# Weight loads of the opening that wait for an earlier landing

## The chip, the cores and the metric

The kernel runs on one core of one Trainium2 chip. The time is device microseconds (us) of one execution. A difference is measured as the median of several runs of each kernel. Beside the times there is a profile of one execution, which records every engine's instructions and every DMA packet.

## The reference

A gated linear recurrence over 768 steps for 4 batches and 8 heads of 48, followed by a feed-forward layer with weights of 384 x 2048 and 2048 x 384. Inputs and weights are drawn in double precision for the weights and in float32 for the rest.

```python
def _attn_ref(q, k, v, alpha):
    B, H, S, D = q.shape                      # 4, 8, 768, 48
    state = np.zeros((B, H, D, D), dtype=np.float32)
    y = np.zeros_like(q)
    for t in range(S):
        state = alpha[:, :, t, :, None] * state + np.einsum('bhd,bhe->bhde', k[:, :, t], v[:, :, t])
        y[:, :, t] = np.einsum('bhd,bhde->bhe', q[:, :, t], state)
    return y

def _moe_ref(x, w_in, w_out):                 # x (3072, 384)
    h = x @ w_in
    g = np.where(h >= 1, h, np.where(h <= -1, 0.0, (h + 1) ** 2 / 4.0))
    return (g @ w_out).astype(np.float32)
```

## The kernel before

The 3072 tokens are cut into 24 chunks of 128 steps, and the chunks into 8 groups of three. For each chunk DVE scans the gates (L478, L485), multiplies keys and queries by the products (L493, L510), TensorE (PE) turns the keys (L574), makes the scores (L589), the state's update (L602) and the outputs (L769). For each group follows one pass of the feed-forward layer: for each of 16 tiles of 128 hidden columns a product with w_in (L878 for group 0, L887 for the others), the activation on ACT and DVE (L918, L928), and a product with w_out (L960 for group 0, L969 for the others). Group 0 multiplies whole float32 numbers; the others use weights split into two parts.

The weights come as 64-bit words and are decoded on the chip. They are loaded in 16 pieces of 768 KB, eight of w_in and eight of w_out, each with two of the 16 tiles, by the function `weights` (the issue is L427). Decoding one piece takes two passes of ACT (L349, L357) and three of DVE (L365, L376, L388), in the piece's own buffer, `wt`. Each piece has a buffer of its own, so a weight load waits for no reader. A chunk needs three loads: the gates `raw_a` (L455, 258.5 KB, two buffers), keys and queries `raw_kq` (L458, 512 KB, two buffers) and values `both` (L465, 512 KB, three buffers); such a load waits until the chunk before it in its buffer has been used. From L402 on the splitting of some weights uses a DMA that adds, issued by POOL.

All loads are issued by SP, in one row, one after the other. An instruction of SP that waits holds up all that stand behind it. The order of all engines is worked out ahead by a planner (`Plan.order`): it gives each operation an engine, a start and an end from costs, and lets a load start only when the transfers before it have at most `DEPTH` = 3 us left to move (with `RATE` = 395 KB per us, about 1.2 MB). The instructions are then emitted in that order at L1043 and L1044, and each engine carries out its own in that order, whenever what it waits for is there. The planned starts themselves do not go into the program.

A load tells of its landing through one of eight semaphores, DMAHW0 to DMAHW7, which the loads take in turn. A load that takes a semaphore whose last user has not been waited for by anyone waits for that user first. So at most eight loads of SP are under way.

The loads of SP are counted here from 1, in SP's order. Load 1 is the first `raw_a`; loads 10, 12, 15, 17, 19, 21, 24, 25, 26, 28, 29, 30, 32, 33, 35 and 36 are the 16 weight loads. Load 22 is a `raw_kq`, loads 23, 27 and 31 are `both`. PE carries out products of zeros (L1020) in the opening, put there by the planner.

Of the kernel before, what the change touches and what calls it, by code (L numbers as in the profile page):

```python
# [29 lines left out]
MORE = 2  # L30
NV = 3
WARM = 10
LAG = 4.0
FETCH = 9
LOAD = 12.0
# [206 lines left out]
def gated_attention_ffn(ctx: ExitStack, tc: tile.TileContext, q, k, v, alpha, w_in, w_out, by, out):  # L242
# [3 lines left out]
    P = 128  # L246
# [57 lines left out]
    with ExitStack() as main:  # L304
# [31 lines left out]
        n_w = NW * DM  # L336
        whole_w = lambda t: t.rearrange("p a m -> p (a m)").bitcast(F32)[:, 0:n_w]

        def decode(u, which, raw, key):

            w = buf("stage", "w", [P, n_w], 2)
            bits = lambda: w().bitcast(I32)


            plan.op(
                "ACT",
                0.92,
                key,
                lambda: nc.scalar.activation(out=w(), in_=word(raw(), F32, 1), func=AF.Copy, scale=2.0**-112),  # L349
                [raw],  # L350
                [w],
            )
            plan.op(
                "ACT",
                0.92,
                key,
                lambda: nc.scalar.activation(out=word(raw(), I32, 0), in_=word(raw(), U32, 0), func=AF.Copy, scale=2.0**-29),  # L357
                [raw],
                [(u, which)],
            )  # L360
            plan.op(
                "DVE",
                0.56,
                key,
                lambda: nc.vector.tensor_scalar(  # L365
                    out=bits(), in0=bits(), scalar1=3, scalar2=None, op0=ALU.logical_shift_left
                ),
                [w],
                [w],
                port=True,  # L370
            )
            plan.op(
                "DVE",
                0.96,
                key,
                lambda: nc.vector.scalar_tensor_tensor(  # L376
                    out=bits(),
                    in0=word(raw(), I32, 1),
                    scalar=-0x80000000,
                    in1=bits(),  # L380
                    op0=ALU.bitwise_and,
                    op1=ALU.bitwise_or,
                ),
                [w, raw],
                [w],
                port=True,
            )
            add = lambda e: e.tensor_tensor(out=whole_w(raw()).bitcast(I32), in0=bits(), in1=word(raw(), I32, 0), op=ALU.add)  # L388
            plan.op("DVE", 0.98, key, lambda: add(nc.vector), [w, raw, (u, which)], [raw], port=True)

        def part_w(u, which, raw, parts, key):
            part = lambda a: parts().rearrange(PARTS[which])[:, a * n_w : (a + 1) * n_w]
            data = lambda: whole_w(raw())
            plan.op("ACT", 0.83, key, lambda: nc.scalar.copy(out=part(0), in_=data()), [raw], [parts])
            sub = lambda e: e.tensor_tensor(out=part(1), in0=data(), in1=part(0).bitcast(F32), op=ALU.subtract)
            if u < BYSUM:
                plan.op("ACT", 0.86, key, lambda: nc.scalar.mul(out=part(1), in_=part(0).bitcast(F32), mul=-1.0), [parts], [parts])
                plan.op(
                    "POOL",
                    1.0,  # L400
                    key,
                    lambda: nc.gpsimd.dma_start(out=part(1), in_=data(), accum_op=ALU.add),  # L402
                    [raw, parts],
                    [parts],
                    moved=P * n_w * 4,
                    land=0.8,
                    rate=Plan.SUM,
                )
                return
            plan.op("DVE", 0.95, key, lambda: sub(nc.vector), [raw, parts], [parts], port=True)  # L410
# [3 lines left out]
        def weights(u):  # L414
# [7 lines left out]
            for k, (t, src) in enumerate(((ti, w_in), (to, w_out))):  # L422
                plan.op(
                    "SP",
                    Plan.ISSUE,
                    fetch[k] + k * LAG,
                    lambda t=t, src=src: nc.sync.dma_start(out=t(), in_=src[u]),  # L427
# [4 lines left out]
            decode(u, "i", ti, ready + off("di", u))  # L432
            decode(u, "o", to, ready + LAG + off("do", u))

        def parts_of(u):
# [4 lines left out]
            part_w(u, "i", raws_w[u][0], wi[u], key + off("wi", u))  # L440
            part_w(u, "o", raws_w[u][1], wo[u], key + LAG + off("wo", u))

# [573 lines left out]
        def fill(n):  # L1016

            idle = pools["ps"].tile([P, 512], F32, name="ps", bufs=8)
            for _ in range(n):
                nc.tensor.matmul(out=idle, lhsT=zeros, rhs=nothing, start=True, stop=True)  # L1020

        plan.op("PE", 0.44 * WARM, -99, lambda: fill(WARM), mode="full")
        for u in range(NU):
# [3 lines left out]
        for j in range(NCH):  # L1027
# [6 lines left out]
            while at < len(segs) and first[at] + groups[at] - 1 <= done:  # L1034
# [3 lines left out]
                for f in range(NF):  # L1038
                    key = begin[at] + f * step[at]
                    second(segs[at], f, hidden(at, f, key), key + LAG)  # L1040
                at += 1
        with tc.manual_schedule():
            for o in plan.order():  # L1043
                o.emit()  # L1044


        near = pools["att"].tile([P, G, P], F32, name="ks", bufs=1)[:, 0, 0 : NCH * G]
# [197 lines left out]
```

## Time and profile before

| | us |
|---|---|
| median of three runs | 501.81 (501.47 to 501.83) |
| the profiled execution | 501.42 |
| its span, first to last instruction | 499.7 |
| PE busy over the span | 491.5 (98%) |
| DVE busy | 347.3 (69%) |
| ACT busy | 317.9 (64%) |

The profiled execution's time is its span and 1.7 us around it; it lies 0.39 us below the median. A share of busy time is a mean over stages. In the opening DVE and the DMA engines are busy nearly all the time, later PE alone is, so a change to the opening has to be read from the opening's own rows.

### The profile page before, as it was taken

What the parts mean: (1) busy time and instruction counts of PE and PEld (TensorE: products, weight loads), DVE (VectorE), ACT (ScalarE), POOL (GpSimd) and SP (SyncE); (2) the same over time, 40 slices, a digit from 0 to 9 for tenths busy, and PEclk for the clock granted to TensorE, in tenths of its full rate; (3) what the DMA queues carried; (4) which work ended last, traced back from release to release, by engine and by line L of the source; (5) the groups of instructions that cost most, each with busy time, mean ns of one, the idle gap of its engine ahead of it and who ended that gap; (6) DMA issues with size and microseconds to landing.
All of it is one profiled execution on the core that took longest, in us unless ns stands there. A gap on an engine that the chain in (4) does not pass through costs nothing.

```text
span 499.7 us, 11372 instructions
## 1 busy us (share of the span) xinstructions
PE 491.5 (98%) x4586; PEld 446.5 (89%) x4586; DVE 347.3 (69%) x609; ACT 317.9 (64%) x603; POOL 30.5 (6%) x70
## 2 busy tenths in 40 slices
PE   8899999999999999999999999999999999999996
PEld 3665656699999999999999999999999999999995
DVE  6998999998997866865866857767755635343332
ACT  3799998998765565565665655665565655555551
POOL 4211102211000000000000000000000000000000
PEclk9999999999999999999999999999999999999999
DMA  8999916878552531542434513434313201001001
GB/s 315 394 387 387 330 23 142 208 201 181 181 159 65 187 102 49 150 137 82 110 95 118 174 47 124 130 100 139 115 35 89 70 1 25 1 7 42 0 1 51
DMA packets 43336, 64.42 MB, mean 129 GB/s; under 512 B 21392, under 2 KB 30736, under 8 KB 43280
## 3 DMA queue, kind: packets, MB, share of 16 engines
q1 hardware_dynamic: 41840, 59.71, 37.4%
q0 software_dynamic: 1440, 3.93, 4.2%
q8 instruction: 38, 0.62, 0.5%
q14 instruction: 18, 0.15, 0.1%
HBM read 48.56 MB, written 9.18 MB: 116 GB/s over the span
## 4 chain that ended last, share of the span: by engine, by line
PE 94%; DVE 3%; issue 1%; DMA 1%; POOL 0%; ACT 0%; DVEq 0%
PE ps L969 36%; PE ps L887 35%; PE ps L878 6%; PE ps L960 6%; PE ps L769 5%; PE ps L602 3%; PE ps L589 2%; DVE inv L485 1%; DVE pre L478 1%; DMA raw_a<-in_al 1%; PE ps L574 1%; DVE inv L493 0%; DVE Q L709 0%; DVE Q L510 0%; DVE state L653 0%
## 5 line engine op out<-in xcount | busy, mean ns | idle before, releaser
L969 PE MATMUL ps<-gh,wt 128*128 128x384 f32 x1008 | 197.1, 340 | 0.0
L887 PE MATMUL ps<-xs,wt 128*128 128x384 f32 x1008 | 193.6, 335 | 0.0
L969 PEld LDWEIGHTS ps<-gh,wt 128*128 128x128 f32 x1008 | 177.7, 188 | 1.3 <-issue 0.2
L887 PEld LDWEIGHTS ps<-xs,wt 128*128 128x128 f32 x1008 | 176.7, 188 | 0.7
L928 DVE SCALAR_TENSOR_TENSOR gf<-gf,ps 128x384 f32<-128x384 f32 x128 | 70.6, 552 | 94.0 <-ACT gf L918 92.5
L918 ACT ACTIVATE gf<-ps,half_b 128x384 f32<-128x384 f32 x128 | 74.4, 582 | 83.4 <-PE ps L887 80.5
L937 ACT CAST gh<-gf 128x384 fp32r<-128x384 f32 x112 | 57.4, 513 | 59.0 <-DVE gf L928 49.7
L938 DVE TENSOR_TENSOR gh<-gf,gh 128x384 fp32r<-128x384 f32 x112 | 62.0, 555 | 33.3 <-ACT gh L937 32.6
L918 ACT ACTIVATE gf<-gf 128x384 f32<-128x384 f32 x128 | 67.2, 525 | 4.0
L635 ACT COPY both<-state 48x192 f32<-48x192 f32 x88 | 30.8, 350 | 10.5 <-PE ps L602 9.1
L960 PE MATMUL ps<-gf,wt 128*128 128x384 f32 x96 | 33.0, 488 | 0.4 <-PE ps L878 0.4
L878 PE MATMUL ps<-xs,wt 128*128 128x384 f32 x96 | 32.7, 489 | 0.1
L478 DVE TENSOR_TENSOR_SCAN pre<-raw_a,fwd 128x516 f32<-128x516 f32 x24 | 29.5, 1228 | 3.0 <-DMA raw_a<-in_al 2.7
L485 DVE TENSOR_TENSOR_SCAN inv<-raw_a,bwd 128x516 f32<-128x516 f32 x24 | 30.1, 1254 | 2.1
L769 PEld LDWEIGHTS ps<-Q,both 128*64 128x64 f32 x368 | 23.2, 138 | 7.2 <-issue 5.6
L960 PEld LDWEIGHTS ps<-gf,wt 128*128 128x128 f32 x96 | 18.0, 190 | 12.4 <-PE ps L878 0.8
L878 PEld LDWEIGHTS ps<-xs,wt 128*128 128x128 f32 x96 | 17.8, 190 | 11.9 <-ACT wt L357 0.4
L769 PE MATMUL ps<-Q,both 128*64 128x64 f32 x368 | 26.6, 225 | 0.0
L769 PE MATMUL ps<-other,both 128*64 128x64 f32 x368 | 26.6, 225 | 0.0
L501 POOL COPY meet<-inv 128x4 f32<-128x4 f32 x24 | 9.8, 408 | 258.3 <-DVE inv L485 258.3
L769 PEld LDWEIGHTS ps<-other,both 128*64 128x64 f32 x368 | 23.2, 138 | 0.0
L709 DVE TENSOR_TENSOR Q<-ps,mask 64x256 f32<-64x256 f32 x48 | 20.3, 423 | 3.6 <-ACT other L672 1.8
(62 smaller groups left out, 370.1 us busy)
## 6 DMA issues: line engine op xcount, KB each, us to landing
raw_kq<-in_kq SPq DMA_DIRECT2D x24, 512.0 KB, 5.2
both<-in_vl SPq DMA_DIRECT2D x24, 512.0 KB, 4.6
raw_a<-in_al SPq DMA_DIRECT2D x24, 258.5 KB, 3.3
wt<-in_w_out SPq DMA_DIRECT2D x8, 768.0 KB, 9.4
wt<-in_w_in SPq DMA_DIRECT2D x8, 768.0 KB, 8.4
out<-ot SPq DMA_DIRECT2D x24, 192.0 KB, 3.1
turned<-w SPq DMA_DIRECT2D x17, 256.0 KB, 2.2
ks<-turned SPq DMA_DIRECT2D x68, 64.0 KB, 2.6
```

The lines of the kernel that those rows point to most:

```text
L478: lambda: nc.vector.tensor_tensor_scan(flat(pre()), a[:, 0:n], flat(fwd), 0.0, ALU.mult, ALU.max),
L485: lambda: nc.vector.tensor_tensor_scan(flat(inv())[:, ::-1], a[:, 1 : n + 1][:, ::-1], flat(bwd)[:, ::-1], 0.0, ALU.mult, ALU.max),
L635: lambda r=r, to=to: nc.scalar.copy(out=to, in_=state[low[r], b]),
L769: nc.tensor.matmul(out=ps()[halves[r], to, halves[u]], lhsT=lhsT[:, u, r], rhs=x()[:, g, halves[u]], start=m + u == 0, stop=True, skip_gro ...
L878: nc.tensor.matmul(out=h(), lhsT=raw_in(f)[:, kt], rhs=whole_x(n)[:, kt].rearrange("p j t -> p (j t)"), start=kt == 0, stop=kt == KT - 1,)
L887: nc.tensor.matmul(out=h(), lhsT=win(f, w)[:, kt], rhs=xs[n]()[:, 0 : groups[n], kt, a], start=(m == 0), stop=(m == 3 * KT - 1),)
L918: lambda: nc.scalar.activation(out=gf(), in_=in_(), func=func, scale=scale, bias=bias),
L928: lambda: nc.vector.scalar_tensor_tensor(out=gf(), in0=gf(), scalar=1.0, in1=h(), op0=ALU.min, op1=ALU.max),
L937: plan.op("ACT", 0.08 + 0.41 * w, key + 0.4, lambda: nc.scalar.copy(out=gh()[:, 0], in_=gf()), [gf], [gh])
L938: sub = lambda e: e.tensor_tensor(out=gh()[:, 1], in0=gf(), in1=gh()[:, 0].bitcast(F32), op=ALU.subtract)
L960: nc.tensor.matmul(out=o_ps[seg][m](), lhsT=raw_out(f)[:, m * P : (m + 1) * P], rhs=gh(), start=f == f0, stop=f == f1 - 1,)
L969: nc.tensor.matmul(out=o_ps[seg][m](), lhsT=wout(f, w)[:, m * P : (m + 1) * P], rhs=gh()[:, a], start=(f == f0 and i == 0), stop=(f == f1 ...
```

## The change

In the loop that emits the planned instructions, each SP operation whose planned start is at most 60 us is looked at. For it the loop collects the SP operations emitted before whose planned landing lies at most 0.3 us after its planned start. If it is a weight load (`moved` is the size of one, P * n_w * 8 bytes), it gets a dependence on the one of these with the latest planned landing: SP waits, by semaphore, until that load has landed. Other loads get no such dependence. No instruction is added to PE, DVE, ACT or POOL, and none is moved; SP has two more semaphore waits that stand alone, since an instruction there carries one wait.

```diff
+QUEUED = 60.0
+WAITS = mybir.DependencyInfo(mybir.DependencyClass.Sync, mybir.DependencyReason.DATA)
...
         with tc.manual_schedule():
+            landed = []
             for o in plan.order():
-                o.emit()
+                made = o.emit()
+                if o.engine != "SP" or o.start > QUEUED:
+                    continue
+                before = [x for x in landed if x[0] <= o.start + 0.3]
+                if before and o.moved == P * n_w * 8:
+                    tc.add_manual_dep(made.ins, max(before, key=lambda x: x[0])[1].name, WAITS, reason="short queue")
+                landed.append((o.end, made.ins))
```

The 16 weight loads wait for these landings (load <- landing waited for): 10 <- 6, 12 <- 8, 15 <- 11, 17 <- 14, 19 <- 15, 21 <- 17, 24 <- 20, 25 <- 22, 26 <- 23, 28 <- 25, 29 <- 26, 30 <- 27, 32 <- 30, 33 <- 31, 35 <- 31, 36 <- 32.

SP, loads 24 to 33, before the change. Numbers behind a name are the buffer's; behind "waits" stand the semaphores, by engine or DMAHW lane.

```order
L427 DMA wt_545<-in_w_out 128x768 [waits DMAHW7_49]
L427 DMA wt_560<-in_w_in 128x768 [waits DMAHW0_49]
L427 DMA wt_577<-in_w_out 128x768 [waits DMAHW1_49]
L465 DMA both_65<-in_vl 128x1024 [waits PE_49,DMAHW2_49,Activation_49,Pool_49]
L427 DMA wt_611<-in_w_in 128x768 [waits DMAHW3_49]
L427 DMA wt_628<-in_w_out 128x768 [waits DMAHW4_49]
L427 DMA wt_639<-in_w_in 128x768 [waits DMAHW5_49]
L465 DMA both_65<-in_vl 128x1024 [waits DMAHW6_49]
L427 DMA wt_666<-in_w_out 128x768 [waits DMAHW7_49]
L427 DMA wt_677<-in_w_out 128x768 [waits DMAHW0_49]
```

The same ten loads after the change (two lines further down in the file).

```order
L429 DMA wt_545<-in_w_out 128x768 [waits DMAHW7_49,DMAHW3_49]
L429 DMA wt_560<-in_w_in 128x768 [waits DMAHW5_49]
L429 DMA wt_577<-in_w_out 128x768 [waits DMAHW6_49,DMAHW1_49]
L467 DMA both_65<-in_vl 128x1024 [waits PE_49,DMAHW2_49,Activation_49,Pool_49]
L429 DMA wt_611<-in_w_in 128x768 [waits DMAHW0_49]
L429 DMA wt_628<-in_w_out 128x768 [waits DMAHW4_49,DMAHW1_49]
L429 DMA wt_639<-in_w_in 128x768 [waits DMAHW2_49]
L467 DMA both_65<-in_vl 128x1024
L429 DMA wt_666<-in_w_out 128x768 [waits DMAHW7_49,DMAHW5_49]
L429 DMA wt_677<-in_w_out 128x768 [waits DMAHW6_49]
```

No load has moved. Before, a weight load waits at most for the load eight places ahead; now it waits for one two to four places ahead (load 25 on lane 5 for load 22, load 28 on lane 0 for load 25). ACT's decode of three of these pieces stands here, unchanged, in both programs:

```order
L394 CAST wt_642<-wt_483 128x768 [waits DVE_49]
L397 ACTIVATE wt_642<-wt_642 128x768 [waits Activation_49]
L349 ACTIVATE w_651<-wt_577 128x768 [waits DMAHW1_49]
L357 ACTIVATE wt_577<-wt_577 128x768
L349 ACTIVATE w_662<-wt_560 128x768 [waits DMAHW0_49,DVE_49]
L357 ACTIVATE wt_560<-wt_560 128x768
L918 ACTIVATE gf_674<-ps_657,half_b_66 128x384 [waits PE_49]
L918 ACTIVATE gf_674<-gf_674 128x384 [waits Activation_49]
L349 ACTIVATE w_679<-wt_628 128x768 [waits DMAHW4_49,DVE_49]
```

The first L349 here reads load 26, the second load 25, the third load 29. Further down, w_789<-wt_698 reads load 35. The first decode of all, w_337<-wt_213, reads load 12.

## Rows read from the trace of the kernel before

**Rows 1.** Chain of waits, 0 to 30 us: shares by line, then start, us, what

```profile
by line: issue 14.3%; DVE inv L485 12.6%; DVE pre L478 12.4%; DMA raw_a<-in_al 9.3%; PE ps L769 5.2%; PE ps L878 5.1%; DVE Q L709 5.1%; DVE inv L493 5.1%; DVE Q L510 4.3%; PE ps L574 4.3%; PE ps L602 4.2%; POOL meet L501 2.4%; DVE state L65
...
0.84 2.80 DMA raw_a<-in_al
...
28.53 1.53 PE ps L878 x4
```

**Rows 2.** Busy time by stretch: stretch, us, engines' busy us (count), PEclk, DMA share, GB/s

```profile
33.10:495.20 462.10, 462.10 (x4114) 428.97 (x4113) 319.10 (x565) 297.54 (x564) 19.51 (x35) 1.00 0.38 112
0.00:33.10 33.10, 29.41 (x473) 17.52 (x474) 27.57 (x44) 20.38 (x40) 10.95 (x35) 1.00 0.95 358
```

**Rows 3.** PE in order of time: start, us, line, operation, [idle before, what ended it]

```profile
18.54 0.78 PE L574 MATMUL ps<-ident,inv 128*128 128x128 f32 x4 [0.89 <-DVE inv L493]
...
24.41 0.63 PE L574 MATMUL ps<-ident,inv 128*128 128x128 f32 x4 [0.69 <-DVE inv L493]
```

**Rows 4.** SP's issues in order of time: start, us (loads 22, 23, 25, 26, 28, 29, 30, 32+33, 35)

```profile
26.00 0.33 SPq L458 DMA_DIRECT2D raw_kq<-in_kq  x1
26.44 0.59 SPq L465 DMA_DIRECT2D both<-in_vl  x1
...
27.72 0.60 SPq L427 DMA_DIRECT2D wt<-in_w_in  x1
28.36 0.49 SPq L427 DMA_DIRECT2D wt<-in_w_out  x1
...
36.80 1.52 SPq L427 DMA_DIRECT2D wt<-in_w_in  x1
38.36 0.43 SPq L427 DMA_DIRECT2D wt<-in_w_out  x1
38.84 0.43 SPq L427 DMA_DIRECT2D wt<-in_w_in  x1
...
39.78 0.94 SPq L427 DMA_DIRECT2D wt<-in_w_out  x2
...
51.66 0.43 SPq L427 DMA_DIRECT2D wt<-in_w_out  x1
```

**Rows 5.** DMA issues, one load a row (22, 23, 25, 26, 28, 29, 30, 32, 35): KB, us to landing

```profile
raw_kq<-in_kq SPq DMA_DIRECT2D x1, 512.0 KB, 8.7
...
both<-in_vl SPq DMA_DIRECT2D x1, 512.0 KB, 9.4
...
wt<-in_w_in SPq DMA_DIRECT2D x1, 768.0 KB, 11.9
...
wt<-in_w_out SPq DMA_DIRECT2D x1, 768.0 KB, 13.2
...
wt<-in_w_in SPq DMA_DIRECT2D x1, 768.0 KB, 7.8
...
wt<-in_w_out SPq DMA_DIRECT2D x1, 768.0 KB, 8.2
...
wt<-in_w_in SPq DMA_DIRECT2D x1, 768.0 KB, 9.6
...
wt<-in_w_out SPq DMA_DIRECT2D x1, 768.0 KB, 14.0
...
wt<-in_w_out SPq DMA_DIRECT2D x1, 768.0 KB, 6.6
```

**Rows 6.** ACT in order of time, first pass of the decode of loads 12, 26, 29, 35

```profile
18.99 0.93 ACT L349 ACTIVATE w<-wt 128x768 f32<-128x768 f32 x1 [0.20 <-DMA wt<-in_w_in]
...
43.81 0.91 ACT L349 ACTIVATE w<-wt 128x768 f32<-128x768 f32 x1
...
49.15 0.89 ACT L349 ACTIVATE w<-wt 128x768 f32<-128x768 f32 x1
...
60.80 0.92 ACT L349 ACTIVATE w<-wt 128x768 f32<-128x768 f32 x1
```

**Rows 7.** DMA issue of POOL's first adding DMA, issued at 44.22 us: KB, us to landing

```profile
wt<-wt POOLq DMA_DIRECT2D x1, 384.0 KB, 9.8
```

## The prediction

> **What bounds the kernel now.** I read the chain of waits first, then busy time by stretch, then PE, SP, the DMA issues and ACT in the opening.
>
> The chain of the first 30 us [rows 1] is to show whether a landing sets anything. It does once: the first gate load, 2.80 us from issue to landing, which is the whole share that DMA has (9.3% of 30 us). No weight load has been issued by then. From 3.64 us the chain runs over DVE (the two scans alone have 25%) and PE, with short pieces of ACT and POOL, and at 28.53 us the first product of the feed-forward part starts. No other landing is among the chain's named shares.
>
> Busy time by stretch [rows 2] says where time can still be won. From 33.10 to 495.20 us PE is busy for 462.10 of 462.10 us. So after 33.1 us nothing can come earlier unless PE's own work shrinks, which the change doesn't touch. Before 33.1 us PE is idle for 33.10 - 29.41 = 3.7 us, and the DMA engines are 95% busy at 358 GB/s. The two larger gaps of PE between its pieces of work in there, 0.89 and 0.69 us, end with DVE's L493, not with a landing [rows 3].
>
> The view of SP's issues with the one of landings [rows 4, 5] is to show in what order the transfers are served. Issue plus time to landing: load 22 at 26.00 + 8.7 = 34.7, load 23 at 26.44 + 9.4 = 35.8, load 25 at 27.72 + 11.9 = 39.6, load 26 at 28.36 + 13.2 = 41.6, load 28 at 36.80 + 7.8 = 44.6, load 29 at 38.36 + 8.2 = 46.6, load 30 at 38.84 + 9.6 = 48.4, load 32 at 39.78 + 14.0 = 53.8. Loads 25 and 26 are issued 0.64 us apart and land 1.9 us apart; 28, 29 and 30 lie 1.56 and 0.48 us apart at issue and 1.9 apart at landing. So loads land in the order of issue, at one 768 KB piece per 1.9 us, however early they were issued: the times to landing of 8 to 14 us are time in a queue. I take that as the rule for the sum: a load lands when its own shortest way is over or when its turn in the queue comes, whichever is later.
>
> **The change part by part.**
>
> Removed: nothing that takes time. The waits for a semaphore's last user (up to eight loads back) give way to waits for nearer loads, and a nearer landing is later, so no weight load can be issued earlier than before. With the order kept, none can then land earlier under the rule above.
>
> Added: sixteen waits on SP. Three questions decide their cost: does the queue run dry, what stands behind the waiting instruction, and who reads the late piece.
>
> Does the queue run dry? The shortest way of a 768 KB load is not in the trace; I estimate it from the first gate load, which found the queue empty: 2.80 us for 258.5 KB [rows 1], plus the other 509.5 KB at 768 KB per 1.9 us, 1.3 us, so 4.1 us. Then, from the landings above:
> load 25 goes out when load 22 lands, at 34.7, and could land at 38.8; its turn was 39.6 (0.8 to spare);
> load 26 after load 23, 35.8, could land at 39.9; turn 41.6 (1.7);
> load 28 after load 25, 39.6, at 43.7; turn 44.6 (0.9);
> load 29 after load 26, 41.6, at 45.7; turn 46.6 (0.9);
> load 32 after load 30, 48.4, at 52.5; turn 53.8 (1.3).
> By the same working the other weight loads with a wait have 0.8 to 3.3 us to spare, or their landing has passed when SP comes to them (loads 12 and 35). So all land where they did, and the cost is 0.
>
> From the other side: a weight issue sometimes takes 1.52 us on SP in place of 0.43 to 0.60 (load 28 [rows 4]), 1.1 us more. If each waited issue did, load 25 would be 0.3 us late, 28, which waits for 25, another 0.2, and 29, behind both, some 0.5. Below nothing the cost could only go if a landing that somebody waits for came sooner; the only such wait that an engine's rows show is ACT's 0.20 us at 18.99 for load 12 [rows 6], whose own issue doesn't move. I take 0, by the row nearest to it, the even 1.9 us between landings.
>
> Who reads the late piece? The decode's first pass on ACT starts, against the landing: load 26 at 43.81, 2.2 us after 41.6; load 29 at 49.15, 2.6 after 46.6; load 35 at 60.80, 2.5 after 51.66 + 6.6 = 58.3 [rows 4 to 6]. These are the three smallest distances after load 12's; the others are 3.4 to 34 us. A lateness of up to 0.5 us ends inside them. This cover is what hides the change; were it gone, each us of lateness would be one us of ACT, and at most one of PE.
>
> What stands behind the waiting instruction? Chunk loads: 22 and 23 now come behind load 21, which waits for load 17's landing at 27.0, so they go out at 27.6 and 28.1 instead of 26.00 and 26.44. Their turns end at 34.7 and 35.8, over 7 us later, so they land as before. Load 31 goes out after load 30 has been released by load 27's landing, some 4 us later than it did; it has no reader before ACT copies a state into that buffer at 59 us, 8 us after its landing. Loads 13, 14, 16, 18, 27 and 34 are held by DVE or PE, not by the weight load ahead.
>
> POOL's adding DMA goes past SP's queue on one of its own and took 9.8 us to land beside a long queue [rows 7]. With a shorter one it may get its share earlier and push loads 29 and 30 back; its share is 384 KB, about 1 us at 1.9 us per 768 KB, 2 us if adding reads and writes. Load 30's reader comes 16 us later, load 29's 2.6. It costs nothing, and its sums are first used at 99 us.
>
> Against the change speaks a rule of the Trainium skill (DMA: Bandwidth & Descriptors, Rules for kernel authors): issue a DMA early and wait for it late, so that its fixed cost overlaps. By that rule each of the waits would expose its load's fixed part. That part is about 2.1 us here (2.80 less 0.65 for the bytes at the rate above), but the two loads still under way cover it. By the rule alone the queue would lose sixteen times that, 34 us; by the landings above, nothing.
>
> The sum: 0 on PE's path. The profiled execution took 501.42 us, 499.7 of span and 1.7 around it; with 0 added it would again take 501.4. The runs' median is 0.39 above that, at 501.81, and I forecast 501.8 for the median.
>
> **The rivals.**
>
> Faster: a short queue lets the loads land sooner, because loads under way share the engines instead of queueing. Then gates and keys of chunks 2 and 3 would land sooner, and the best it could do is close the two gaps of PE before 28.5 us, 0.89 + 0.69 = 1.6 us: 500.2. For it speaks that DMA is 95% busy; against it, the even landings, and that both gaps end with DVE, which waits for no landing after the first. In the same direction points the skill's figure for HBM latency (DMA: Bandwidth & Descriptors, Latency and other measured facts: 0.2 us on average, 2 us under high load). By it a load might land up to 1.8 us sooner after its last byte, which no row of the first 33 us turns into time beyond ACT's 0.20 us.
>
> Slower: the queue runs dry at loads 25 to 29, because a load issued on a landing still needs what load 28 needed with three loads ahead of it, 7.8 us, and not 4.1. Then load 25 lands at 42.5, load 26 at 43.6, load 28 at 50.3, load 29 at 51.4. Load 29's decode, due at 49.15, starts 2.2 us late, ACT does its work in order, and PE waits as long: 504.0. It decides from a lateness of 2.6 us at load 29, or 2.2 at load 26. For it speaks that no weight load here was issued to an empty queue, so 4.1 is an estimate; against it, that load 28's 7.8 us are explained by its turn.
>
> The change doesn't act: the waits are over when SP reaches them. Where that holds (two loads) it costs 0, and it gives the same 501.8.
>
> **How the numbers follow.** The three runs before span 0.36 us, so I take 0.2%, 1.0 us, as what can be told from no change. My forecast with the waits that don't act: 0.85, all of it within 0.2%. The faster rival: 0.07, the slower one: 0.08, each counted whole on its side. The forecast's own spread is the runs' (501.5 to 501.8) and 0.5 us of lateness if it all came through, 501.3 to 502.3. The range takes in about half of the way to the bound of 0.2% beyond that: 501.0 to 502.6.
>
> **What would show it.** SP issues load 25 at about 34.7, 28 at 39.6 and 29 at 41.6, and the time to landing of the weight loads falls to about 5 or 6 us, while the landings stay within 0.5 us of 39.6, 44.6 and 46.6. The first product starts at 28.5, and PE has no gap from 33.1 us on. I am wrong if the first product moves by more than 0.5 us, if load 26 lands after 43.8 or load 29 after 49.1, or if PE shows an idle stretch before L878 or L960 between 33 and 100 us that ends with ACT's or DVE's decode.

## The result, and the profile after

The changed kernel takes 503.96 us (median of six runs, 503.32 to 506.46), the kernel before 501.59 (six runs, 501.42 to 501.83). The ratio is 1.006, with an interval of 1.0047 to 1.0074: 2.4 us slower. The forecast was 501.8.

The profiled execution is the longest of the six, 506.46 us with a span of 504.7, so it shows more than the median lost: 5.0 us of span. Its mean granted clock is 0.994, that of the four shorter runs 0.998 to 1.0. PE in order of time (start, us, line, operation, [idle before, what ended it]):

```profile
7.25 0.63 PE L576 MATMUL ps<-ident,inv 128*128 128x128 f32 x4 [1.66 <-POOL meet L503]
...
19.17 0.63 PE L576 MATMUL ps<-ident,inv 128*128 128x128 f32 x4 [1.48 <-DVE inv L495]
...
30.00 4.11 PE L880 MATMUL ps<-xs,wt 128*128 128x384 f32 x12
34.70 0.48 PE L962 MATMUL ps<-gf,wt 128*128 128x384 f32 x1 [0.59 <-PE ps L880]
...
72.05 0.91 PE L962 MATMUL ps<-gf,wt 128*128 128x384 f32 x2 [1.30 <-DVE gf L930]
...
82.40 0.33 PE L576 MATMUL ps<-ident,inv 128*128 128x128 f32 x1 [0.41 <-DVE inv L495]
...
96.05 0.63 PE L576 MATMUL ps<-ident,inv 128*128 128x128 f32 x4 [0.94 <-DVE xs L811]
```

Two places lose time. The first feed-forward product starts at 30.00 instead of 28.53 us [rows 1], 1.5 us later. And between 70 and 96 us PE, which had no idle time at all from 33.1 us on before [rows 2], has three gaps of together 2.65 us. The rest, under 1 us, is spread over shorter delays.

The gaps go back to one wait of ACT. Who waited for whom from 60 to 75 us (us in total, times, longest), and ACT's rows at loads 29 and 35:

```profile
ACT w L351 <- DMA wt<-in_w_out: 5.4, 1, 5.4
DVE w L367 <- ACT w L351: 4.0, 2, 3.8
POOL other L693 <- ACT other L683: 3.1, 1, 3.1
PEld ps L962 <- DVE gf L930: 1.9, 1, 1.9
PE ps L962 <- DVE gf L930: 1.3, 1, 1.3
```

```profile
51.04 0.91 ACT L351 ACTIVATE w<-wt 128x768 f32<-128x768 f32 x1 [0.18 <-DMA wt<-in_w_out]
...
67.77 0.90 ACT L351 ACTIVATE w<-wt 128x768 f32<-128x768 f32 x1 [5.38 <-DMA wt<-in_w_out]
```

The row at 67.77 is the decode of load 35, which started at 60.80 without a wait [rows 6]. ACT works in order, so everything behind it, the activations among them, is late too; DVE waits for ACT and PE for DVE.

SP's issues of loads 25, 28, 29, 30, 32 with 33, and 35, and the time to landing of 25, 26, 28, 29, 30, 32 and 35 answer to [rows 4, 5]:

```profile
37.02 0.33 SPq L429 DMA_DIRECT2D wt<-in_w_in  x1
...
42.37 0.33 SPq L429 DMA_DIRECT2D wt<-in_w_in  x1
44.92 0.33 SPq L429 DMA_DIRECT2D wt<-in_w_out  x1
46.10 0.33 SPq L429 DMA_DIRECT2D wt<-in_w_in  x1
...
54.73 2.31 SPq L429 DMA_DIRECT2D wt<-in_w_out  x2
...
57.56 0.61 SPq L429 DMA_DIRECT2D wt<-in_w_out  x1
```

```profile
wt<-in_w_in SPq DMA_DIRECT2D x1, 768.0 KB, 5.3
...
wt<-in_w_out SPq DMA_DIRECT2D x1, 768.0 KB, 6.3
...
wt<-in_w_in SPq DMA_DIRECT2D x1, 768.0 KB, 6.1
...
wt<-in_w_out SPq DMA_DIRECT2D x1, 768.0 KB, 6.0
...
wt<-in_w_in SPq DMA_DIRECT2D x1, 768.0 KB, 8.6
...
wt<-in_w_out SPq DMA_DIRECT2D x1, 768.0 KB, 6.0
...
wt<-in_w_out SPq DMA_DIRECT2D x1, 768.0 KB, 10.1
```

Issue plus time to landing gives 42.3 for load 25 (39.6 before), 48.5 for 28 (44.6), 50.9 for 29 (46.6), 54.7 for 30 (48.4), 60.7 for 32 (53.8) and 67.7 for 35 (58.3). The lateness grows: 2.7, 3.9, 4.3, 6.3, 6.9, 9.4 us. Some 1.3 us of it were there before any weight load waited (load 9 landed at 14.76 instead of 13.42): in this execution load 4 (`raw_a` of chunk 1, issued at 2.21) took 6.9 us to land instead of 5.5, and DVE's scan waited 1.40 us for it:

```profile
9.11 1.23 DVE L480 TENSOR_TENSOR_SCAN pre<-raw_a,fwd 128x516 f32<-128x516 f32 x1 [1.40 <-DMA raw_a<-in_al]
```

That is a chance of this execution (in the other profiles here load 4 lands between 7.1 and 8.7 us, in this one at 9.1). The growth beyond it comes with the waits; the kernel with the later waits alone, below, shows it without this chance.

Busy time by stretch (stretch, us, engines' busy us, PEclk, DMA share, GB/s), first the kernel before, then the changed one:

```profile
34.00:44.00 10.00, 10.00 (x60) 6.06 (x59) 9.31 (x14) 9.74 (x15) 0.00 (x0) 1.00 1.02 412
```

```profile
20.86:24.28 3.42, 3.42 (x74) 2.94 (x71) 2.47 (x4) 3.15 (x6) 0.28 (x2) 0.50 1.04 421
...
34.00:44.00 10.00, 9.41 (x58) 5.86 (x58) 9.32 (x14) 9.61 (x17) 0.00 (x0) 1.00 0.92 316
```

The same ten us move 412 GB/s before and 316 after. (The share adds up the times of the packets and passes 1 where packets overlap.) Some of that is engines without work (share 0.92 against 1.02), but more is that the packets themselves take longer: those of the weight loads in this stretch 294 ns in the mean against 242.

From 20.86 to 24.28 us PE also ran at 1.2 GHz (granted clock 0.50) in this execution, after gaps of 1.66 and 1.48 us. The first product's 1.5 us are this stretch and the 0.63 us by which L576 was late at 19.17 (18.54 before [rows 3]), behind the scan that waited for load 4; no weight load's wait stands in front of them. So the opening's share of the loss is probably larger here than in the median run.

### The profile page after: what moved, and what is told of

It is laid out like the page before. It is cut to its first block, busy times and chain, and to the rows that moved or that the text cites. A ratio compares the mean times of both kernels' runs of the same rounds, so it can differ in the third digit from the quotient of the medians.

```text
span 504.7 us, 11374 instructions
## 1 busy us (share of the span) xinstructions
PE 492.1 (98%) x4586; PEld 447.3 (89%) x4586; DVE 347.5 (69%) x609; ACT 316.8 (63%) x603; POOL 30.6 (6%) x70
## 4 chain that ended last, share of the span: by engine, by line
PE 87%; DVE 4%; DMA 3%; ACT 3%; issue 1%; SPq 0%; DVEq 0%; ACTq 0%
PE ps L971 36%; PE ps L889 35%; PE ps L771 5%; PE ps L962 3%; PE ps L880 3%; PE ps L604 2%; PE ps L591 2%; DMA wt<-in_w_out 2%; DMA raw_a<-in_al 1%; DVE pre L480 1%; ACT w L351 1%; ACT wt L359 1%; ACT gf L920 1%; DVE inv L487 0%; PE ps L576 0%
## 5 line engine op out<-in xcount | busy, mean ns | idle before, releaser
L962 PE MATMUL ps<-gf,wt 128*128 128x384 f32 x96 | 33.1, 489 | 1.9 <-DVE gf L930 1.3
```

Source lines behind the costliest of these rows:

```text
L962: nc.tensor.matmul(out=o_ps[seg][m](), lhsT=raw_out(f)[:, m * P : (m + 1) * P], rhs=gh(), start=f == f0, stop=f == f1 - 1,)
```

## The experiments

The theories: **A**, the queue runs dry again and again (too little is under way, though the engines are seldom idle), so the lateness adds up until load 35 is later than its 2.5 us of cover; **B**, the early waits delay the chunk loads behind them and so the first product; **C**, a wait on SP costs by itself.

**Waits in the early part alone.**

```diff
-                if before and o.moved == P * n_w * 8:
+                if before and o.moved == P * n_w * 8 and o.start < 23.0:
```

> Only the five weight loads with a planned start under 23 us keep their wait (10, 12, 15, 17, 19); the later eleven are issued as before the change. Theory A (the queue runs dry again and again, the lateness adds up to load 35, whose decode ACT waits for): the later loads catch up in a long queue, load 35 lands within 1.5 us of 58.2 and ACT doesn't wait for it; median 501.4 to 502.2. Rival B (the early waits delay the chunk loads behind them and so the first feed-forward product): first product at 29.5 to 30 instead of 28.5, 502.8 to 504.0.

Measured: 501.47 us against 501.31, ratio 1.0003 (0.9993 to 1.0013). PE's first product and ACT's decode of load 35 in order of time, then the time to landing of load 35:

```profile
28.42 4.11 PE L880 MATMUL ps<-xs,wt 128*128 128x384 f32 x12
...
60.81 0.92 ACT L351 ACTIVATE w<-wt 128x768 f32<-128x768 f32 x1
```

```profile
wt<-in_w_out SPq DMA_DIRECT2D x1, 768.0 KB, 7.2
```

The first product starts where it did and ACT doesn't wait. B falls for these five waits by themselves.

**Waits in the later part alone.**

```diff
-                if before and o.moved == P * n_w * 8:
+                if before and o.moved == P * n_w * 8 and o.start > 23.0:
```

> Only the eleven weight loads with a planned start over 23 us keep their wait (21, 24, 25, 26, 28 to 30, 32, 33, 35, 36). Theory A: load 35 lands at 64 to 68, ACT waits 2 to 5 us for it, PE has gaps of 1 to 3 us between 65 and 100 us; 503.0 to 504.3. Rival B: the first product starts at 28.5 and the time is that of before, 501.4 to 502.0.

Measured: 503.58 us, ratio 1.0041 (1.0025 to 1.0057). In order of time SP's issue of load 35, ACT's decode of it and PE's gap behind it:

```profile
55.48 0.43 SPq L429 DMA_DIRECT2D wt<-in_w_out  x1
...
66.43 0.90 ACT L351 ACTIVATE w<-wt 128x768 f32<-128x768 f32 x1 [5.75 <-DMA wt<-in_w_out]
...
70.68 0.59 PE L962 MATMUL ps<-gf,wt 128*128 128x384 f32 x1 [1.64 <-DVE gf L930]
```

The stretch shown above, in this kernel:

```profile
34.00:44.00 10.00, 10.00 (x61) 6.07 (x60) 9.23 (x15) 9.73 (x15) 0.00 (x0) 1.00 0.96 337
```

The time to landing of load 35:

```profile
wt<-in_w_out SPq DMA_DIRECT2D x1, 768.0 KB, 10.9
```

Its first product starts at 28.46 and its clock stays at 2.4 GHz until the end of PE's work, and the loss is there all the same: load 35 lands at 66.4. Its interval overlaps that of the whole change, so these eleven waits account for most or all of the loss. Single runs go from 501.31 to 505.59, much further apart than before the change (501.00 to 503.15 in 30 runs); probably the loads are not equally late in every run, but only one was profiled.

**No waits from load 32 on.**

```diff
-QUEUED = 60.0
+QUEUED = 46.0
```

> The weight loads 10 to 30 keep their wait, loads 32, 33, 35 and 36 have none. Theory A, with most of the lateness made at loads 32 and 33, which find an empty queue: load 35 lands at 60 to 63, ACT waits under 2 us for it, 501.6 to 502.6. If the lateness is already made by loads 25 to 30: load 35 lands after 63, 502.8 to 504. Rival B: as the changed kernel, 503.3 to 504.5.

Measured: 501.83 us, ratio 1.0011 (0.9995 to 1.0027), not told apart from no change. In its profile load 35 lands 7.6 us after its issue at 53.87, at 61.5, and its decode at 63.01 doesn't wait. PE and ACT in order of time, then load 35's time to landing:

```profile
26.30 0.38 PE L1022 MATMUL ps<-zeros 128*128 128x512 bf16 x1 [1.33 <-issue]
...
30.96 4.03 PE L880 MATMUL ps<-xs,wt 128*128 128x384 f32 x12
...
63.01 0.91 ACT L351 ACTIVATE w<-wt 128x768 f32<-128x768 f32 x1
```

```profile
wt<-in_w_out SPq DMA_DIRECT2D x1, 768.0 KB, 7.6
```

The decode was due later in this execution, since its first product started at 30.96 us, after a gap of 1.33 us of PE that the trace puts down to issue and 3.4 us at 1.2 GHz; so the median says more than the profile here. The whole 2.4 us that its span is longer is this late first product; PE has no idle time behind 35.3 us. Load 35 is 3.3 us late here, 9.4 in the changed kernel. By this and the median, most of the lateness that decides is made from load 32 on; the waits of loads 10 to 30 alone stay inside the cover or nearly so.

**A deeper queue.** The landing waited for is one planned 3 us earlier (about 2.4 MB under way), and in a further kernel 1.5 us earlier (1.8 MB):

```diff
-                before = [x for x in landed if x[0] <= o.start + 0.3]
+                before = [x for x in landed if x[0] <= o.start - 2.7]
```

> Every weight load waits as in the change, but for a landing planned 3 us earlier, so that about 2.4 MB are under way instead of 1.2. Theory A: the queue no longer runs dry, landings within 1 us of those before the change, 501.4 to 502.0. Rival C (a wait on SP costs by itself, in SP's time or in what stands behind it, however early the landing): 502.8 to 504.

Measured: 501.38 us, ratio 1.0001 (0.9992 to 1.0011). Load 35 lands at 52.00 + 6.6 = 58.6. Its decode, its time to landing, and the stretch shown above:

```profile
61.09 0.92 ACT L351 ACTIVATE w<-wt 128x768 f32<-128x768 f32 x1
```

```profile
wt<-in_w_out SPq DMA_DIRECT2D x1, 768.0 KB, 6.6
```

```profile
34.00:44.00 10.00, 10.00 (x60) 6.06 (x59) 9.36 (x14) 9.53 (x15) 0.00 (x0) 1.00 0.99 389
```

All sixteen loads still depend on an earlier landing, six of loads 24 to 35 (24, 25, 26, 30, 32 and 33) go out within 0.1 us of it, so that SP does wait, and the time is that of before. C falls.

For the kernel with 1.8 MB:

> Waits as in the change, for a landing planned 1.5 us earlier, so that about 1.8 MB are under way. Theory A (the cost is the lateness of load 35 beyond 2.5 us, made by a queue that runs dry): load 35 lands within 2 us of 58.2, ACT waits under 0.5 us for it, 501.2 to 502.0. If the loss grew evenly with the depth taken away (1.2 MB: 2.4 us, 2.4 MB: 0): 502.5.

Measured: 501.54 us against 501.41, ratio 1.0003 (0.9994 to 1.0013); load 35 lands at 51.93 + 6.8 = 58.7, and its decode doesn't wait:

```profile
61.02 0.92 ACT L351 ACTIVATE w<-wt 128x768 f32<-128x768 f32 x1
```

```profile
wt<-in_w_out SPq DMA_DIRECT2D x1, 768.0 KB, 6.8
```

The loss does not grow evenly as depth is taken away. It can't be told from nothing at 1.8 MB and is 2.4 us at 1.2 MB. These sizes are the planner's. By the issues and landings in the traces, what was still to land when one of the loads 24 to 35 of weights went out was 3.5 MB in the mean before, 1.3 MB in the changed kernel, and 2.5 and 1.8 MB in these two.

**Load 35 ahead of load 32.** All waits of the change; the pieces of loads 32 and 35 change places in the emitted order.

```diff
+            order = plan.order()
+            loads = [i for i, o in enumerate(order) if o.engine == "SP" and o.moved == P * n_w * 8]
+            a, b, c = loads[-4:-1]
+            oa, ob, oc = order[a], order[b], order[c]
+            oa.start, oa.end, oc.start, oc.end = oc.start, oc.end, oa.start, oa.end
+            order[a], order[c] = oc, oa
-            for o in plan.order():
+            for o in order:
```

> All waits of the change, 1.2 MB under way; only the pieces of loads 32 and 35 change places on SP (32's piece is decoded 31 us after its landing, 35's 2.5 us). Theory A with load 35's decode as the only place that costs: the piece that was load 35 lands at 57 to 61, ACT waits under 1 us, 501.2 to 502.2, although the queue runs dry as often. If lateness costs at several places: 502.5 to 504.

Measured: 501.66 us, ratio 1.0014 (0.9999 to 1.0029). The piece lands 5.5 us after its issue at 54.26, at 59.8, and its decode follows at 61.95 without a wait. PE and ACT in order of time, then the piece's time to landing:

```profile
26.50 0.38 PE L1022 MATMUL ps<-zeros 128*128 128x512 bf16 x1 [1.06 <-issue]
...
29.66 4.03 PE L880 MATMUL ps<-xs,wt 128*128 128x384 f32 x12
...
61.95 0.92 ACT L351 ACTIVATE w<-wt 128x768 f32<-128x768 f32 x1
```

```profile
wt<-in_w_out SPq DMA_DIRECT2D x1, 768.0 KB, 5.5
```

The load now in place 35 lands at 68.0, as late as ever, but it is the piece whose decode comes near 86 us. The same stretch moves 328 GB/s, and PE has no idle time behind 34.3 us. A queue that is just as dry costs at most 0.3% once the piece with the small cover isn't at its end. Load 35's decode is the place of the median's loss.

Something is left for single executions: two of these ten runs took over 503 us (504.08 and 504.33), three of the ten without waits from load 32 on (up to 504.38), one of 49 of the kernel before. In the profile here the whole 1.0 us that the span is longer is the first product's, at 29.66 instead of 28.53, again after a gap of PE put down to issue. In all three profiles of kernels that keep both the early waits and those of loads 21 to 30, the first product comes 1.1 to 2.4 us late, though with either half alone it doesn't. Whether the waits together make it so isn't shown; by the medians it is worth less than 0.3%.

**One load at a time.** Each weight load waits for the load right ahead of it.

```diff
-                before = [x for x in landed if x[0] <= o.start + 0.3]
+                before = landed[-1:]
```

> Each weight load of the opening waits for the landing of the load right ahead of it, so it finds an empty queue: this measures its shortest way, which the prediction put at 4.1 us. If the prediction's estimate holds and the 5.3 to 8.6 us in the changed kernel came from what was still ahead: median 4.0 to 4.5 us to landing. If the way itself is longer, because a landing is that of the slowest of the 16 engines: 5 to 6.5 us. The time is 510 to 540 either way.

Measured in one run: 532.4 us. The issues of L429 (duration in ns, minimum, median, maximum) and their time to landing:

```profile
L429 SPq DMA_DIRECT2D wt<-in_w_out x8: 327/328/328, 14.3 to 89.5; - x8
L429 SPq DMA_DIRECT2D wt<-in_w_in x8: 327/328/328, 19.1 to 93.8; - x8
...
DMA to landing us min/median/max: 4.1/4.3/5.8
```

The way of a load by itself is 4.3 us in the median and 4.1 at the least, so the prediction's estimate of 4.1 was right, and the other expectation, a longer way of each load by itself, fell. The long ways in the changed kernel are not made by one load alone.

## Why the prediction was wrong

Right: what bounds the kernel (PE without idle time from 33.1 us on, so that nothing behind could come earlier), landings in the order of issue, the shortest way of 4.1 us, no cost of a wait as such. The first product's start was right for either half of the waits (28.42 and 28.46); in the changed kernel's profile it moved by 1.5 us, for which load 4 and the clock account.

The step that failed is the answer to "does the queue run dry?", with its rule that a load lands when its own shortest way is over or when its turn comes. The turns were taken from the landings before, one 768 KB piece per 1.9 us, and with 0.8 to 1.7 us to spare all loads were to land where they did. That pace belongs to a queue that never runs dry. With 1.2 MB under way it fell from 412 to 316 GB/s, 337 in the kernel with the later waits alone. Each load then released the next one late, and what was to spare was gone by load 25: loads 25, 28 and 29 were put at 34.7, 39.6 and 41.6 us on SP and went out at 37.0, 42.4 and 44.9 (some 1.3 us of that by the chance at load 4). In the kernel with the later waits alone load 25 went out at 34.1, in time, and still landed 1.3 us late.

The rule itself fails too, not only the turns put into it. With the issues and landings measured in that kernel, 4.1 us for a load's way and 1.9 us for a turn, load 33 should land at 59.4 and load 35 at 64.2 us; they landed at 61.7 and 66.4.

The second part of the step was to follow the lateness to load 29 only and to bound it at 0.5 us. The cover of 2.5 us at load 35 was named, but nothing was added up along loads 30, 32 and 33, the weakest stretch: load 32 goes out when load 30 lands, with one load of 512 KB left ahead of it. In the kernel with the later waits loads 25, 28 and 32 were 1.3, 2.0 and 3.8 us late and load 35 was 8.1 us late, against a cover of 2.5.

The slower rival had the right chain (decode, ACT in order, PE), but the wrong place and the wrong cause, so that its price, 504.0, fits by luck: it had ACT wait 2.2 us at load 29 for a way of 7.8 us. Load 29's decode waited 0.18 us, load 35's 5.38. It was given 0.08, because the even landings of the kernel before were read as a property of the engines and not of the depth of the queue that they were measured in.

The faster rival had nothing for it: no kernel with waits was faster than the one before, at any depth.

The rule that was weighed there, of the Trainium skill (DMA: Bandwidth & Descriptors, Rules for kernel authors), to issue early and wait late, pointed the right way. The trace agrees in the direction; of the reason, the fixed part of a load, it shows a sign at load 32 alone, which in the kernel with the later waits took 4.5 us, about as long as a load by itself (4.3), and landed 2.9 us behind load 31. At the other late loads the pace of the queue came to the fore.

What stays open is why the pace falls, and how the lateness of 8 us divides. POOL's adding DMAs run in the same time (one from 44.15 to 53.99 us in the kernel with the later waits, the next from 56.76 to 66.58) and take a share of the engines just when loads 30 to 35 are late. The first of them took as long before the change (44.22 to 54.05), the second only 6.3 us; so neither got through sooner beside a short queue, which the prediction had thought possible. A kernel without them would have needed other work on DVE and another order, and wasn't tried.

## What to carry to other kernels

A landing rate read from a queue that is always full holds for a full queue; before a load is made to wait for another's landing, allow for a lower one and add the lateness up to the last load, not to the next. Compare that sum with the smallest distance between a landing and its reader, wherever in the chain it stands. Here half as much again under way (1.8 MB in place of 1.2) cost nothing that could be told, and neither did moving the one piece with a small cover ahead of one that could wait.

## What the runs showed of the hardware

Packets of the weight loads, 6144 bytes each, took 246 ns in the mean before and at 2.4 MB under way, 283 ns in the changed kernel, and 296 ns with one load at a time (means over the 2048 packets of each trace). In the last, the first 16 of a piece's 128 packets took 542 ns in the mean and the last 16 took 242: a piece that finds the engines idle starts slowly. That can't be all of the fall in pace: in the changed kernel the first 16 took 343 ns and the last 16 took 334 (253 and 262 before). Why some packets are slow was not tested.

The gap of PE that two profiles put down to issue comes with a late packet of instructions. A 16 KB packet of them (DMA queue 8) starts at 23.96 and 24.20 us there, and at 22.50 to 23.06 in the five profiles whose first product is at most 0.3 us late. In all seven PE's product of zeros that follows (L1020, L1022) starts 2.3 to 2.6 us behind the packet. PE may have waited for its instructions; that was not tested.
